# A long convolution with soft mixture-of-experts on one core: token sums in column quarters, combination in row quarters, experts with moving weights, spread weight loads

## The chip, the cores and the metric

The kernel runs on one NeuronCore of one Trainium2 chip, in f32 throughout. The metric is the device time of one execution in microseconds. Before the change it is 1391.36 us, the median of three runs (1389.31 to 1397.85).

## The reference

```python
def _attn_ref(x, h):                        # x (8, 5696, 128), h (5696, 128)
    Yf = np.fft.rfft(x, n=2 * S, axis=1) * np.fft.rfft(h, n=2 * S, axis=0)[None]
    return np.fft.irfft(Yf, n=2 * S, axis=1)[:, :S, :]

def _moe_ref(x, phi, w1, w2):               # x (45568, 128): 8 experts, 4 slots each, F = 1024
    logits = x @ phi                        # (45568, 32)
    d = softmax over the tokens (axis 0);  slot_input = d.T @ x
    slot_out[e] = relu(slot_input[e] @ w1[e]) @ w2[e]
    c = softmax over the slots (axis 1);   return c @ slot_out
```

(The two softmaxes are cut to a line each; both subtract the maximum and add 1e-9 to the sum.)

## The kernel before, in words

The convolution is a transform in two factors, 90 by 64, written as matmuls. The sequence is 89 rows of 64 columns (`R1 = 89`, `N2 = 64`), and a chunk is four columns from one end and the four mirrored ones from the other (`CH = 4`), so a batch has 8 chunks (`NJ`) and all of x has 64. The stages of the front are `stage_a` (matmul at L175, its result through DRAM as `f`), `stage_b1` (L205, the product with the transform of h on VectorE) and `stage_b2` (L241, its result through DRAM as `z`). `load_z` (L269) brings z back, `stage_c1` (L278) makes the convolved tokens y of a chunk, `stage_c2` transposes them (L295), `stage_c3` makes the logits (L303) and the token-wise softmax numerators, `stage_c4` transposes the combination weights and stores them to DRAM as `c_t` (L337, L342). Two chunks are a window: `window_max`, `window_top` (L358) and `window_row` (L376) keep a running maximum per slot over the tokens, and from it come the numerators d (L386, L389).

`dispatch` (from L394) sums d times y over the tokens of a chunk. Its weights are the 128 columns (4 token columns by 32 slots) of d, its moving operand the 512 columns (4 token columns by 128 channels) of y; only the four diagonal blocks of the 128 by 512 product are of use. A second matmul (L408) with the same weights and a column of ones gives the sums of d. At the end of a window five operations on VectorE (L418) merge the diagonal blocks and the sums into `acc`.

The order is written out by hand: the loop over `t` issues the pieces of several chunks in turn, with lags. The front runs in the steps t = 0 to 80, the token sums of chunk c in step t = c + 29, so that steps 29 to 80 hold both and steps 81 to 92 hold the token part alone. All loads and stores but four go through SyncE's queue (SP) in program order, eight of them in flight at most.

In step 81 (`t == last_front`) the front's memory is given back and all weights of the experts are loaded there, sixteen DMAs of 512 KB (L514, L515). After the loop the combination weights come back from DRAM (`cT`, L522, eight DMAs). The experts (L548, L556) take the weights `w1s` and `w2s` as stationary operand, 128 by 128 at a time, and 4 slots as moving operand. The result is spread into `sobd`, a block-diagonal operand of 128 by 512, and for each chunk two matmuls of 512 columns (L584) over 128 rows (4 token columns by 32 slots) give the output, which ScalarE and VectorE copy (L591, L589) and SP stores (L597).

Of the kernel before, what the change touches and what calls it, by code (L numbers as in the profile page):

```python
# [56 lines left out]
def kernel(  # L57
# [63 lines left out]
    aps = work.enter_context(tc.tile_pool(name="aps", bufs=1, space=PSUM))  # L121
# [131 lines left out]
    ybufs = [ypool.tile([P, 2 * CH, D], F32, name=f"y{i}") for i in range(NYB)]  # L253
# [19 lines left out]
    def stage_c1(c):  # L273
# [10 lines left out]
        nc.vector.tensor_tensor(out=y_[0:R1, 0:CH, :], in0=pv[0], in1=yo[:, :, :], op=AL.add)  # L284
        nc.vector.tensor_tensor(out=y_[0:R1, CH:2 * CH, :], in0=pv[0], in1=yo[:, :, :],
# [3 lines left out]
    def stage_c2(c):  # L289
        yt = cpool.tile([D, 2 * CH, R1], F32, name="yt", tag="yt")  # L290
        for f in range(2):
            p = bank()
            pv = p[:, 0:CH * R1].rearrange("p (n r) -> p n r", r=R1)
            for i in range(CH):
                nc.tensor.transpose(pv[:, i, :], ys[c][0:R1, f * CH + i, :], ident[0:R1, 0:R1])  # L295
            nc.scalar.activation(yt[:, f * CH:(f + 1) * CH, :], pv, AF.Copy)  # L296
        yts[c] = yt
# [96 lines left out]
    def dispatch(c):  # L394
        w, i = divmod(c, WC)
        if i == 0:
            accs[w] = (aps.tile([P, 512], F32, name="ap", tag="ap"),
                       aps.tile([P, 512], F32, name="sp", tag="sp"))
        ap_, sp_ = accs[w]
        d_ = ds.pop(c)  # L400
        y_ = ys.pop(c)
        for f in range(2):
            dv = d_[:, f * CH:(f + 1) * CH, :].rearrange("p n s -> p (n s)")
            first, last = i == 0 and f == 0, i == WC - 1 and f == 1
            nc.tensor.matmul(ap_[:, :], dv,  # L405
                             y_[:, f * CH:(f + 1) * CH, :].rearrange("p n d -> p (n d)"),
                             start=first, stop=last)
            nc.tensor.matmul(sp_[:, 0:1], dv, ones[:, 0:1], start=first, stop=last)  # L408
        if i < WC - 1:
            return  # L410
        parts = [(slice(q * NSL, (q + 1) * NSL), slice(0, D), ap_[q * NSL:(q + 1) * NSL,
                                                               q * D:(q + 1) * D])
                 for q in range(Q)] + [(slice(0, P), slice(D, D + 1), sp_[:, 0:1])]
        for r, cl, src in parts:
            if w == 0:
                nc.vector.tensor_copy(out=acc[r, cl], in_=src)
            else:
                nc.vector.scalar_tensor_tensor(out=acc[r, cl], in0=acc[r, cl],  # L418
                                               scalar=scales[w][r, 0:1], in1=src,
                                               op0=AL.mult, op1=AL.add)  # L420
# [27 lines left out]
    wait_b2 = []  # L448

    for t in range(steps):  # L450
# [57 lines left out]
        if t == last_front:  # L508
# [10 lines left out]
    tail = work.enter_context(tc.tile_pool(name="tail", bufs=1))  # L519
    cT = tail.tile([P, B * NJ, 2, R1], F32, name="cT")  # L520
    for b in range(B):
        nc.sync.dma_start(out=cT[:, b * NJ:(b + 1) * NJ, :, :].rearrange("p j f r -> p (j f r)"),  # L522
                          in_=cd[:, b * NJ:(b + 1) * NJ, :, :].rearrange("p j f r -> p (j f r)"))


    rep = wts.tile([P, NSL], F32, name="rep")
    for q in range(Q):
        r = slice(q * NSL, (q + 1) * NSL)
        nc.vector.tensor_copy(out=rep[r, :], in_=ident[r, r])
    p = bank()  # L530
    nc.tensor.matmul(p[0:NSL, 0:D + 1], rep[:, :], acc[:, :], start=True, stop=True)
# [9 lines left out]
    siT = wts.tile([P, NSL], F32, name="siT")  # L541
    nc.vector.tensor_copy(out=siT[:, :], in_=p[:, 0:NSL])
    hT = wts.tile([P, E, NFC, SPE], F32, name="hT")
    for e in range(E):
        hp = bank()
        hv = hp[:, 0:NFC * SPE].rearrange("p (t s) -> p t s", s=SPE)
        for k in range(NFC):
            nc.tensor.matmul(hv[:, k, :], w1s[:, e, k * P:(k + 1) * P],  # L548
                             siT[:, e * SPE:(e + 1) * SPE], start=True, stop=True)
        nc.scalar.activation(hT[:, e, :, :], hv, AF.Relu)  # L550
    soT = tail.tile([P, NSL], F32, name="soT")
    for e0 in range(0, E, 4):
        pp = [bank() for _ in range(4)]
# [4 lines left out]
        for e in range(e0, e0 + 4):  # L558
            nc.vector.tensor_copy(out=soT[:, e * SPE:(e + 1) * SPE], in_=pp[e - e0][:, 0:SPE])
    p = bank()  # L560
    nc.tensor.transpose(p[0:NSL, 0:D], soT[:, :], ident[:, :])
    so = tail.tile([NSL, D], F32, name="so")
    nc.vector.tensor_copy(out=so[:, :], in_=p[0:NSL, 0:D])
    rep2 = tail.tile([NSL, Q, NSL], F32, name="rep2")
    for q in range(Q):
        nc.vector.tensor_copy(out=rep2[:, q, :], in_=ident[0:NSL, 0:NSL])
    sobd = tail.tile([P, 2, Q, D], F32, name="sobd")
    nc.gpsimd.memset(sobd[:, :, :, :], 0.0)
    p = bank()
    nc.tensor.matmul(p[:, 0:D], rep2[:, :, :].rearrange("p q s -> p (q s)"), so[:, :],  # L570
                     start=True, stop=True)
    for q in range(Q):
        r = slice(q * NSL, (q + 1) * NSL)
        nc.vector.tensor_copy(out=sobd[r, 0, q, :], in_=p[r, 0:D])
        nc.scalar.activation(sobd[r, 1, Q - 1 - q, :], p[r, 0:D], AF.Copy)

    osp = work.enter_context(tc.tile_pool(name="osb", bufs=4))
    ov = out.rearrange("(b a n) d -> b a n d", b=B, n=N2)
    for c in range(B * NJ):
        b, j = divmod(c, NJ)  # L580
        o_ = osp.tile([R1, 2, CH, D], F32, name="o", tag="o")
        for f in range(2):
            p = bank()
            nc.tensor.matmul(p[0:R1, :], cT[:, c, f, :],  # L584
                             sobd[:, f, :, :].rearrange("p q d -> p (q d)"),
                             start=True, stop=True)
            pv = p[0:R1, :].rearrange("p (n d) -> p n d", d=D)
            if f:
                nc.vector.tensor_copy(out=o_[:, f, :, :], in_=pv)  # L589
            else:  # L590
                nc.scalar.activation(o_[:, f, :, :], pv, AF.Copy)  # L591
        gap = N2 - CH * (2 * j + 1)
        for r in (slice(0, SPLIT), slice(SPLIT, R1)):
# [33 lines left out]
```

## Time and profile before

| | us |
|---|---|
| median of 3 runs | 1391.36 |
| profiled execution | 1390.6 |
| its span | 1388.6 |
| PE busy | 1288.8 |
| VectorE busy | 732.7 |
| ScalarE busy | 501.1 |
| GpSimd busy | 306.2 |

PE is TensorE's matmuls, PEld its weight loads, which run beside matmuls. A group line gives line, engine, operation, result and operands, shapes (weights as rows*columns, then the moving operand), count, busy time, mean duration of one, and idle time before. Matmuls are pipelined: a duration includes the way through the array, so the spacing of matmuls is the busy time divided by the count. PEclk is the granted TensorE clock as a share of full speed, and the DMA share is the mean busy share of the 16 DMA engines.

### The profile page before, as it was taken

The numbers are of one execution on the slowest core, as the hardware profiler recorded it, in microseconds if no ns is written. First come the engines' busy times: TensorE is split into PE (matmuls) and PEld (weight loads), VectorE is DVE, ScalarE is ACT, GpSimd is POOL, SyncE is SP. The second block draws the span as 40 slices with busy tenths as digits, with TensorE's granted clock in tenths as the row PEclk, the third lists the DMA queues.
The fourth block names the chain that finished last, engine by engine and source line by source line (L and its number), as shares of the span: only waits on it lengthen the run. The fifth ranks groups of instructions, "written<-read, shape, count | busy, mean of one in ns | idle before, by whom it ended". The sixth has DMA issues, their size and how long they took to land.

```text
span 1388.6 us, 17824 instructions
## 1 busy us (share of the span) xinstructions
PE 1288.8 (93%) x5408; PEld 819.4 (59%) x5408; DVE 732.7 (53%) x1722; ACT 501.1 (36%) x1118; POOL 306.2 (22%) x346
## 2 busy tenths in 40 slices
PE   7588899999999999999999999999999659799998
PEld 2254565666666666666666666666676435496333
DVE  2045555665666666566666665666776424401443
ACT  3365343434343434433443334333333213101333
POOL 5233222222222322322232222221111101100000
PEclk9899999999999999999999999999999878756999
DMA  7799898877777677687767778766655753311776
GB/s 198 234 271 272 266 281 250 272 202 222 215 212 209 191 214 214 193 229 217 203 200 213 215 200 218 219 200 175 178 159 158 210 156 80 120 60 43 216 213 203
DMA packets 197532, 277.73 MB, mean 200 GB/s; under 512 B 18072, under 2 KB 134040, under 8 KB 197439
## 3 DMA queue, kind: packets, MB, share of 16 engines
q1 hardware_dynamic: 196863, 276.14, 68.2%
q8 instruction: 45, 0.74, 0.2%
q10 hardware_dynamic: 576, 0.46, 0.1%
q14 instruction: 48, 0.39, 0.1%
HBM read 147.09 MB, written 129.43 MB: 199 GB/s over the span
## 4 chain that ended last, share of the span: by engine, by line
PE 82%; DMA 8%; DVE 4%; SPq 2%; ACT 1%; issue 1%; POOL 1%; POOLq 0%; ACTq 0%; DVEq 0%
PE bank L278 17%; PE bank L175 15%; PE bank L205 11%; PE bank L241 10%; PE bank L584 8%; PE ap L405 7%; PE bank L303 5%; PE bank L295 3%; DMA gt<-f 3%; DMA f<-fst 2%; PE bank L556 2%; PE bank L548 2%; DMA zc<-z 1%; SPq L514 1%; PE sp L408 1%
## 5 line engine op out<-in xcount | busy, mean ns | idle before, releaser
L175 PE MATMUL bank<-x,s 128*128 128x512 f32 x576 | 283.5, 618 | 12.2 <-POOL x L164 6.9
L278 PE MATMUL bank<-zc,i 128*128 128x512 f32 x512 | 238.8, 610 | 23.1 <-DMA zc<-z 23.1
L205 PE MATMUL bank<-gt,wt 128*128 128x256 f32 x810 | 216.0, 390 | 27.5 <-DMA gt<-f 26.8
L164 POOL TENSOR_TENSOR x<-xc 89x512 f32<-89x512 f32 x144 | 182.4, 1267 | 219.4 <-PE bank L175 168.7
L177 ACT ACTIVATE fst<-bank 90x512 f32<-90x512 f32 x288 | 160.1, 587 | 173.5 <-PE bank L175 61.9
L205 PEld LDWEIGHTS bank<-gt,wt 128*128 128x128 f32 x810 | 152.2, 193 | 116.6 <-issue 82.2
L223 DVE TENSOR_TENSOR pr<-bank,Hr 128x512 f32<-128x512 f32 (+1 forms) x184 | 124.1, 674 | 170.8 <-PE bank L205 170.8
L241 PE MATMUL bank<-yf,vt 128*128 128x256 f32 x720 | 187.0, 381 | 5.9 <-DVE yf L229 4.3
L244 ACT ACTIVATE zst<-bank 128x512 f32<-128x512 f32 (+1 forms) x184 | 107.3, 583 | 227.9 <-PE bank L241 175.9
L278 PEld LDWEIGHTS bank<-zc,i 128*128 128x128 f32 x512 | 94.1, 194 | 121.9 <-issue 89.2
L175 PEld LDWEIGHTS bank<-x,s 128*128 128x128 f32 x576 | 103.8, 195 | 99.4 <-issue 78.6
L284 DVE TENSOR_TENSOR y<-bank,yo 89x512 f32<-89x512 f32 x64 | 44.0, 687 | 213.1 <-PE bank L278 198.9
L317 POOL TENSOR_TENSOR ct<-L,rm 89x256 f32<-89x256 f32 x64 | 39.2, 612 | 530.0 <-DVE rm L315 391.8
L241 PEld LDWEIGHTS bank<-yf,vt 128*128 128x128 f32 x720 | 136.6, 191 | 29.6 <-issue 6.1
L405 PE MATMUL ap<-y,d 128*128 128x512 f32 x256 | 144.0, 651 | 2.5 <-ACT d L389 2.5
L223 DVE TENSOR_TENSOR pi<-bank,Hi 128x512 f32<-128x512 f32 (+1 forms) x184 | 122.9, 668 | 0.0
L584 PE MATMUL bank<-sobd,cT 128*89 128x512 f32 x256 | 111.5, 598 | 2.4 <-issue 2.4
L303 PEld LDWEIGHTS bank<-phi,yt 128*89 128x89 f32 x1024 | 91.0, 159 | 9.6 <-issue 3.8
L408 PEld LDWEIGHTS sp<-ones,d 128*128 128x128 f32 x256 | 51.1, 200 | 65.6 <-issue 65.6
L303 PE MATMUL bank<-phi,yt 128*89 128x32 f32 x1024 | 88.4, 240 | 0.3 <-ACT yt L296 0.3
L227 DVE TENSOR_TENSOR yf<-pr,pi 128x256 f32<-128x256 f32 (+1 forms) x184 | 82.1, 446 | 6.4
L584 PEld LDWEIGHTS bank<-sobd,cT 128*89 128x89 f32 x256 | 40.8, 160 | 72.5 <-issue 72.2
(77 smaller groups left out, 1133.3 us busy)
## 6 DMA issues: line engine op xcount, KB each, us to landing
f<-fst SPq DMA_DIRECT2D x144, 360.0 KB
gt<-f SPq DMA_DIRECT2D x396, 128.0 KB
zc<-z SPq DMA_DIRECT2D x64, 720.0 KB
z<-zst SPq DMA_DIRECT2D x176, 256.0 KB
xc<-in_x_dram SPq DMA_DIRECT2D x64, 320.0 KB
out_dram<-o SPq DMA_DIRECT2D x64, 320.0 KB
c_t<-cst SPq DMA_DIRECT2D x64, 89.0 KB
cT<-c_t SPq DMA_DIRECT2D x8, 712.0 KB
```

What stands on the lines that cost most here:

```text
L164: nc.gpsimd.tensor_tensor(out=y_[0:R1, :, :], in0=t_[:, 0, :, :], in1=t_[:, 1, ::-1, :], op=AL.subtract if comp else AL.add)
L175: nc.tensor.matmul(p[:, :], s1[:, tab[G], :], src[:, :, :].rearrange("p n d -> p (n d)"), start=True, stop=True)
L177: nc.scalar.activation(st[:, :, G, :], p[0:N1, :].rearrange("p (n d) -> p n d", d=D), AF.Copy)
L205: nc.tensor.matmul(p[:, q * 256:(q + 1) * 256], wt[:, 2 * i + q, :], t_[:, q, :, :].rearrange("p c d -> p (c d)"), start=True, stop=True)
L223: nc.vector.tensor_tensor(out=t[:, 0:n, :, :], in0=pv[:, 0:n, :, :], in1=H[:, 2 * i:2 * i + n, :].unsqueeze(2).broadcast_to([P, n, 2, D]), ...
L227: nc.vector.tensor_tensor(out=y_[:, 0:n, 0, :], in0=pr[:, 0:n, 0, :], in1=pi[:, 0:n, 1, :], op=AL.subtract)
L241: nc.tensor.matmul(p[:, q * 256:(q + 1) * 256], vt[:, 2 * i + q, :], y_[:, q, :, :].rearrange("p c d -> p (c d)"), start=True, stop=True)
L244: nc.scalar.activation(st[:, 0:n, :], p[:, 0:n * 256].rearrange("p (q c) -> p q c", q=n), AF.Copy)
L278: nc.tensor.matmul(p[:, :], i1[:, tabs[q], :], t_[:, o, :, q, :], start=(q == 0), stop=(q == 1))
L303: nc.tensor.matmul(p[0:R1, i * NSL:(i + 1) * NSL], yt[:, i, :], phi[:, :], start=True, stop=True)
L405: nc.tensor.matmul(ap_[:, :], dv, y_[:, f * CH:(f + 1) * CH, :].rearrange("p n d -> p (n d)"), start=first, stop=last)
L584: nc.tensor.matmul(p[0:R1, :], cT[:, c, f, :], sobd[:, f, :, :].rearrange("p q d -> p (q d)"), start=True, stop=True)
```

## The change

**Token sums in column quarters.** The rows of y get one more column, set to 1 once (`D + 1` = 129 wide). Each of the four token columns becomes a matmul of its own with 32 columns of d as weights, whose result goes to its own 32 partitions of one bank: column quarters of the array. The diagonal blocks alone are computed, the ones column gives the sums, and one operation merges a window. The bank is now double.

**Weight loads spread.** w1 and w2 of one expert are loaded at the end of each of the steps 81 to 88, with the combination weights of one batch in each of the steps 81 to 87; the last batch follows after the loop.

**Experts with moving weights.** The slot inputs are laid out with zeros (`siz`), 32 columns per expert in which only the expert's own 4 are filled, and are the stationary operand, with w1 moving, 512 columns at a time; four experts go to four column quarters. The hidden layer is transposed on PE, and its 32-column pieces are the weights against which w2 moves, 128 columns at a time.

**Combination in row quarters.** The slot outputs stand four times, once per 32 partitions (`so4`). For each token column a matmul over 32 rows, with 89 columns of `cT` as weights and 128 moving columns, writes to one of four banks: row quarters of the array. Two chunks go together, with one copy per bank.

```diff
-    aps = work.enter_context(tc.tile_pool(name="aps", bufs=1, space=PSUM))
+    aps = work.enter_context(tc.tile_pool(name="aps", bufs=2, space=PSUM))
...
-    ybufs = [ypool.tile([P, 2 * CH, D], F32, name=f"y{i}") for i in range(NYB)]
+    ybufs = [ypool.tile([P, 2 * CH, D + 1], F32, name=f"y{i}") for i in range(NYB)]
...
+    for t_ in ybufs:
+        nc.vector.memset(t_[0:R1, :, D:D + 1], 1.0)
...
         for f in range(2):
-            dv = d_[:, f * CH:(f + 1) * CH, :].rearrange("p n s -> p (n s)")
-            first, last = i == 0 and f == 0, i == WC - 1 and f == 1
-            nc.tensor.matmul(ap_[:, :], dv,
-                             y_[:, f * CH:(f + 1) * CH, :].rearrange("p n d -> p (n d)"),
-                             start=first, stop=last)
-            nc.tensor.matmul(sp_[:, 0:1], dv, ones[:, 0:1], start=first, stop=last)
+            for q in range(Q):
+                nc.tensor.matmul(ap_[q * NSL:(q + 1) * NSL, 0:D + 1], d_[:, f * CH + q, :],
+                                 y_[:, f * CH + q, :], start=(i == 0 and f == 0),
+                                 stop=(i == WC - 1 and f == 1))
...
+            nc.vector.scalar_tensor_tensor(out=acc[:, :], in0=acc[:, :],
+                                           scalar=scales.pop(w)[:, 0:1], in1=ap_[:, 0:D + 1],
+                                           op0=AL.mult, op1=AL.add)
...
-            for e in range(E):
-                nc.sync.dma_start(out=w1s[:, e, :], in_=moe_w1[e])
-                nc.sync.dma_start(out=w2s[:, e, :, :],
-                                  in_=moe_w2[e].rearrange("(c p) d -> p c d", p=P))
+        e = t - last_front
+        if 0 <= e < E:
+            nc.sync.dma_start(out=w1s[:, e, :], in_=moe_w1[e])
+            nc.sync.dma_start(out=w2s[:, e, :, :],
+                              in_=moe_w2[e].rearrange("(c p) d -> p c d", p=P))
+            if e < B - 1:
+                load_c(e)
...
-        for k in range(NFC):
-            nc.tensor.matmul(hv[:, k, :], w1s[:, e, k * P:(k + 1) * P],
-                             siT[:, e * SPE:(e + 1) * SPE], start=True, stop=True)
...
+            for q in range(Q):
+                nc.tensor.matmul(p[q * NSL:(q + 1) * NSL, :], siz[:, g * Q + q, :],
+                                 w1s[:, g * Q + q, f0:f0 + FH], start=True, stop=True)
...
+                nc.tensor.transpose(p[:, k * P:(k + 1) * P],
+                                    hid[:, g, (k0 + k) * P:(k0 + k + 1) * P], ident[:, :])
...
         for k in range(NFC):
-            for e in range(e0, e0 + 4):
-                nc.tensor.matmul(pp[e - e0][:, 0:SPE], w2s[:, e, k, :], hT[:, e, k, :],
-                                 start=(k == 0), stop=(k == NFC - 1))
+            for q in range(Q):
+                nc.tensor.matmul(sop[q * NSL:(q + 1) * NSL, 0:D],
+                                 hidT[:, g, k, q * NSL:(q + 1) * NSL], w2s[:, g * Q + q, k, :],
+                                 start=(g == 0 and k == 0), stop=(g == EG - 1 and k == NFC - 1))
...
-        for f in range(2):
-            p = bank()
-            nc.tensor.matmul(p[0:R1, :], cT[:, c, f, :],
-                             sobd[:, f, :, :].rearrange("p q d -> p (q d)"),
-                             start=True, stop=True)
+        pq = [bank() for _ in range(Q)]
+        for i in range(PC):
+            for f in range(2):
+                k = (i * 2 + f) * D
+                for q in range(Q):
+                    r = slice(q * NSL, (q + 1) * NSL)
+                    nc.tensor.matmul(pq[q][0:R1, k:k + D], cT[r, c0 + i, f, :], so4[r, :],
+                                     start=True, stop=True)
```

The order of the program shows at three places what moves. First TensorE in a combined step, around one dispatch (`ap` is the bank of the token sums, `sp` that of the sums of d, `y` and `d` a chunk's tokens and numerators; the shape is that of the result). Before:

```order
L303 MATMUL bank<-phi,yt 89x32 x8
L175 MATMUL bank<-x_99,s_92 128x512 x2
L205 MATMUL bank<-gt,wt 128x256 x2
L241 MATMUL bank<-yf,vt 128x256 x2
L337 MATMUL bank<-ident,ct 128x89 x2
L405 MATMUL ap<-y_104,d_110 128x512
L408 MATMUL sp<-ones,d_110 128x1
L405 MATMUL ap<-y_104,d_110 128x512
L408 MATMUL sp<-ones,d_110 128x1
L175 MATMUL bank<-x_98,s_92 128x512 x2
L205 MATMUL bank<-gt,wt 128x256 x2
```

And with the change:

```order
L305 MATMUL bank<-phi,yt 89x32 x8
L175 MATMUL bank<-x_99,s_92 128x512 x2
L205 MATMUL bank<-gt,wt 128x256 x2
L241 MATMUL bank<-yf,vt 128x256 x2
L339 MATMUL bank<-ident,ct 128x89 x2
L405 MATMUL ap<-y_104,d_110 32x129 x8
L175 MATMUL bank<-x_98,s_92 128x512 x2
L205 MATMUL bank<-gt,wt 128x256 x2
```

Four matmuls of a dispatch have become eight smaller ones; everything around them stands as it did (line numbers move by two).

Second, SyncE's queue from step 81 on (`zc` is z coming back, `c_t` the store of combination weights, `w1s` and `w2s` the experts' weights). Before, from the middle of the sixteen weight loads:

```order
L514 DMA w1s<-in_moe_w_dram 128x1024
L515 DMA w2s<-in_moe_w_dram 128x8x128
L514 DMA w1s<-in_moe_w_dram 128x1024
L515 DMA w2s<-in_moe_w_dram 128x8x128
L514 DMA w1s<-in_moe_w_dram 128x1024
L515 DMA w2s<-in_moe_w_dram 128x8x128
L269 DMA zc_107<-z 90x2x1024
L342 DMA c_t<-cst 128x178
L269 DMA zc_106<-z 90x2x1024
L342 DMA c_t<-cst 128x178
```

And with the change, from the first of them:

```order
L344 DMA c_t<-cst 128x178
L518 DMA w1s<-in_moe_w_dram 128x1024
L519 DMA w2s<-in_moe_w_dram 128x8x128
L447 DMA cT<-c_t 128x1424
L271 DMA zc_107<-z 90x2x1024
L344 DMA c_t<-cst 128x178
L518 DMA w1s<-in_moe_w_dram 128x1024
L519 DMA w2s<-in_moe_w_dram 128x8x128
L447 DMA cT<-c_t 128x1424
L271 DMA zc_106<-z 90x2x1024
```

Each z load now has three loads ahead of it in its step, where one had sixteen and the others none; the reads of `cT` have moved from behind the loop into the steps.

Third, TensorE from the last dispatch to the end. Before:

```order
L408 MATMUL sp<-ones,d_108 128x1
L531 MATMUL bank<-acc,rep 32x129
L540 MATMUL bank<-ident,si 128x32
L548 MATMUL bank<-siT,w1s 128x4 x64
L556 MATMUL bank<-hT,w2s 128x4 x64
L561 MATMUL bank<-ident,soT 32x128
L570 MATMUL bank<-so,rep_10157 128x128
L584 MATMUL bank<-sobd,cT 89x512 x128
```

And with the change:

```order
L405 MATMUL ap<-y_105,d_108 32x129 x8
L534 MATMUL bank<-acc,rep_10075 32x129
L543 MATMUL bank<-ident,si 128x32
L559 MATMUL bank<-w1s,siz 32x512 x16
L570 MATMUL bank<-ident,hid 128x128 x16
L578 MATMUL ap<-w2s,hidT 32x128 x64
L584 MATMUL bank<-so,rep_10075 128x128
L600 MATMUL bank<-so_10214,cT 89x128 x512
```

64 matmuls of 4 columns against w1 have become 16 of 512 and 16 transposes, the 64 against w2 are now 128 columns wide, and the combination has 512 matmuls of 128 columns in place of 128 of 512.

More of the change, by code (lines that the diff above doesn't have):

```diff
@@ L396, in dispatch @@
         if i == 0:
[L397 to L399 removed]
+            accs[w] = aps.tile([P, 512], F32, name="ap", tag="ap")
+        ap_ = accs[w]
         d_ = ds.pop(c)
@@ L561 @@
[L561 to L568, printed above, removed]
-    p = bank()
-    nc.tensor.matmul(p[:, 0:D], rep2[:, :, :].rearrange("p q s -> p (q s)"), so[:, :],
-                     start=True, stop=True)
```

118 lines of the change are left out of this document (66 added, 52 removed).

## The prediction

> **What bounds the kernel now.** I read the page first, then busy time by stretches, then groups by shape, then the chain of waits and the timelines. The profiled execution took 1390.6 us (span 1388.6 us and 2.0 us around it); the median of the three runs shown is 1391.36 us, so the sum below starts from 1390.6. About 1% (14 us) is what a measurement of this kernel can tell from no change.
>
> The page: busy time, then in 40 slices the TensorE clock that was granted and the DMA share.
>
> ```profile
> span 1388.6 us, 17824 instructions
> PE 1288.8 (93%) x5408; PEld 819.4 (59%) x5408; DVE 732.7 (53%) x1722; ACT 501.1 (36%) x1118; POOL 306.2 (22%) x346
> ...
> PEclk9899999999999999999999999999999878756999
> DMA  7799898877777677687767778766655753311776
> ```
>
> PE is the bound on average, but the clock sags between slices 31 and 36, so the end of the program must be read apart from its middle. Busy time by stretches does that:
>
> ```profile
> core 0: us, PE busy (x) PEld busy (x) DVE busy (x) ACT busy (x) POOL busy (x), PEclk, DMA share, GB/s
> 1091.11:1123.75 32.64, 9.91 (x48) 5.67 (x45) 6.62 (x21) 4.11 (x12) 3.23 (x5) 0.65 1.04 302
> 1123.75:1183.90 60.15, 55.01 (x261) 33.51 (x262) 26.65 (x74) 15.42 (x41) 10.15 (x16) 0.87 0.28 74
> 1183.90:1209.30 25.40, 21.33 (x91) 12.34 (x89) 7.93 (x26) 6.13 (x17) 6.14 (x9) 0.82 0.19 66
> 1213.35:1240.47 27.12, 27.12 (x129) 27.12 (x129) 0.00 (x0) 1.38 (x7) 0.00 (x0) 0.51 0.25 103
> 1240.47:1267.80 27.33, 27.31 (x128) 27.22 (x128) 1.13 (x7) 0.20 (x1) 0.00 (x0) 0.50 0.00 1
> 1272.29:1383.90 111.61, 111.51 (x256) 40.77 (x256) 43.28 (x63) 38.13 (x65) 0.00 (x0) 0.99 0.69 203
> 230.00:1071.00 841.00, 833.40 (x3854) 554.73 (x3853) 537.12 (x1265) 326.05 (x727) 210.94 (x246) 1.00 0.72 206
> ```
>
> Four stages, four limits. In 230 to 1071 (the 52 steps, t = 29 to 80, in which the front and the token sums run together) PE works 833 of 841 us at full clock: PE time taken away there comes off the end. In 1091 to 1124 the DMA engines are full (1.04, 302 GB/s) and PE works 9.9 of 32.6 us. In 1213 to 1268 (experts) PE is busy throughout, at half clock, with nothing moving. In the combination from 1272 PE is busy throughout and the DMA engines at 0.69.
>
> **The prices.** Groups by shape; count, then busy us and mean ns of one:
>
> ```profile
> L405 PE MATMUL ap<-y,d 128*128 128x512 f32 x256 | 144.0, 651 | 2.5 <-ACT d L389 2.5
> L584 PE MATMUL bank<-sobd,cT 128*89 128x512 f32 x256 | 111.5, 598 | 2.4 <-issue 2.4
> L303 PE MATMUL bank<-phi,yt 128*89 128x32 f32 x1024 | 88.4, 240 | 0.3 <-ACT yt L296 0.3
> ...
> L548 PE MATMUL bank<-siT,w1s 128*128 128x4 f32 x128 | 27.1, 351 | 0.3 <-DVE siT L542 0.3
> ```
>
> The code issues 128 matmuls on L584 and the trace has 256: each f32 matmul is two passes, each with its own weight load. A pass of 512 columns costs 111.5/256 = 0.436 us, 0.85 ns a column: 0.110 us for 129 columns, 0.109 for 128. L548 is bound by its weight loads: 27.1/128 = 0.212 us for 128 columns at clock 0.51, so 0.83 ns a column at full clock, 0.027 us for 32. L303 gives at most 88.4/1024 = 0.086 us for a load of 89 columns and L548's rate 0.074: I take 0.08.
>
> What no row shows is two passes at once on different quarters of the array. The ends are: none at all, and four at a time. Between them I take this mechanism: the two passes of one matmul use the same quarter and follow each other, while the second pass of one runs beside the first of the next matmul, which sits on another quarter, once that one's weights are in. A matmul then costs one pass and one weight load instead of two passes. I choose it because in all these rows PE takes instructions in program order, and that order puts both passes of a quarter together.
>
> **Token sums.** One dispatch now, in the chain of waits:
>
> ```profile
> 1131.16 0.89 PE ap L405 x2
> 1132.06 0.12 PE sp L408 x2
> 1132.17 0.97 PE ap L405 x2
> 1133.14 0.12 PE sp L408 x2
> ```
>
> That is 2.10 us. After, 8 matmuls of 129 columns on 32-column weights: 8 x (0.110 + 0.027) = 1.10 us; no overlap gives 16 x 0.110 = 1.76, or 2.19 if the small weight loads stop being hidden too; four at a time gives a quarter of 1.76 and some 0.1 to start, 0.55. I take 1.10: 1.00 us off each of 52 PE-bound steps, **52 us** (ends -5 and 81). The single merge in place of five on DVE and the 129-wide rows of y lie on an engine that works 537 of 841 us: nothing, covered by PE; without that cover the wider rows still move the same 512 elements.
>
> A rule speaks against this part. The row first: an L405 pass occupies 0.56 us of PE (144.0/256) but is recorded as 651 ns, and L584's 0.436 as 598, so up to 0.16 us of a pass drains beside its successor. The Trainium skill, TensorEngine Tiling (Array Packing), Key Properties, states that changing the tiling mode drains TensorE; no run here shows it yet. By that rule each of the two switches of a dispatch would expose this drain; without it the sum stays as it is.
>
> **Last steps.** PE's timeline at the first and last combined step, and SP's issue of the z load between:
>
> ```profile
> 1091.11 3.63 PE L278 MATMUL bank<-zc,i 128*128 128x512 f32 x8
> ...
> 1123.75 6.01 PE L278 MATMUL bank<-zc,i 128*128 128x512 f32 x8 [21.43 <-DMA zc<-z]
> ...
> 1183.91 4.90 PE L278 MATMUL bank<-zc,i 128*128 128x512 f32 x8
> ```
>
> ```profile
> 1112.58 2.49 SPq L269 DMA_DIRECT2D zc<-z  x1
> ```
>
> The z load stands behind the sixteen weight loads on SP, issues at 1112.6, 21 us after the first step began, and PE idles 21.4 us for it. These seven steps take 92.8 us. Sizes:
>
> ```profile
> zc<-z SPq DMA_DIRECT2D x64, 720.0 KB
> ...
> out_dram<-o SPq DMA_DIRECT2D x64, 320.0 KB
> c_t<-cst SPq DMA_DIRECT2D x64, 89.0 KB
> cT<-c_t SPq DMA_DIRECT2D x8, 712.0 KB
> w1s<-in_moe_w_dram SPq DMA_DIRECT2D x8, 512.0 KB
> w2s<-in_moe_w_dram SPq DMA_DIRECT2D x8, 512.0 KB
> ...
> out_dram<-o SPq DMA_DIRECT2D x64, 36.0 KB
> ```
>
> After, each step moves 512 + 512 + 712 + 720 + 89 KB = 2.6 MB, at 302 GB/s 8.6 us. The z load now waits on SP behind one w1, one w2 and one cT load, and behind it stand the c_t store and the next step's loads; PE waits for z. I allow 1 us for it to land: 9.6 us a step, against PE's own 10.0 (60.15/6, at clock 0.87) less the dispatch's 1.0. So DMA sets it: 7 x 9.6 = 67 us, **25 us** saved (ends: 9, if load and clock dips add up to 12 us a step; 30, if PE's 9.0 holds). The four dispatches after 1183.9 give 1 us each, **4 us**. The cT loads moved forward were hidden behind the experts and save nothing by themselves: their 5.8 MB take 19 us at 302 GB/s, and 31 us of experts would still cover that.
>
> **Experts.** From the last dispatch (1209.3) to the first combination matmul (1272.3) it is 63 us. After: the same 4 us to the slot inputs; 16 matmuls of 512 columns, 16 x (0.436 + 0.027) = 7.4; an eviction 0.9; 16 transposes x 0.109 = 1.7; an eviction 0.9; 64 x (0.109 + 0.027) = 8.7; copies and the replication 1.6: 25 us at full clock. The clock was 0.82 before this stage and 0.50 in it, so I add 6 us for a slow first third: 31, **32 us** saved. Without overlap PE takes 14 + 14 and the stage 43; with full overlap 21.
>
> **Combination.** From 1272.3 to the end is 116.3 us, 4.8 of it outside PE's 111.5. After, 512 matmuls of 128 columns on 89-column weights: 512 x (0.109 + 0.08) = 97, with 4.8 it is 101.6: **15 us** saved. No overlap: 1024 x 0.109 = 111.6, nothing. Full overlap: 1024 weight loads x 0.08 = 82, 30 us. Two other floors lie below: 64 x 356 KB = 23.3 MB at 302 GB/s is 77 us, and evictions and issues:
>
> ```profile
> L597 SPq DMA_DIRECT2D out_dram<-o x128: 317/340/436, 1276.4 to 1385.0; - x128
> L591 ACT ACTIVATE o<-bank x64: 592/593/593, 1274.3 to 1383.0; 89x512 f32<-89x512 f32 x64
> L589 DVE COPY o<-bank x64: 686/687/690, 1275.7 to 1383.9; 89x512 f32<-89x512 f32 x64
> ```
>
> 64 x 0.687 = 44 us on DVE, 128 x 0.34 = 44 us on SP. A new wait: each pair of chunks takes four of six banks, so the next pair's third matmul waits for the first eviction. A pair's PE time (3.0 us) covers the two evictions of each engine (1.4 us); at four at a time it would not, and about 0.7 us per pair shows, still under the weight loads.
>
> **The sum.** 52 + 25 + 4 + 32 + 15 = 128 us: 1390.6 - 128 = **1263 us**.
>
> **Rivals.**
> 1. Four quarters at a time: 81 + 31 + 42 + 30 = 184, **1207 us**. For it: a weight load already runs inside another pass (the L584 loads are 40.8 us within 111.5). Against: both passes of a quarter stand together in program order. The Trainium skill, TensorE: Matmul & The Clock Gate, Measured speedup vs the span model, gives 2.38 for three column tiles and 3.07 for four row tiles, without saying that this holds for two-pass f32; no row here shows it. Chance 0.20.
> 2. Quarters do not overlap: 18 (0.34 x 52) + 26 + 20 + 0 = 64, **1327 us**. For it: every row now is one pass behind the other. Chance 0.22.
> 3. Overlap as forecast, but each switch of shape drains the array: 64 dispatches x 2 x 0.16 = 21 us, **1284 us**. Chance 0.12.
> 4. Slower: the combination runs at half clock. In the expert windows PE is busy throughout and still granted 0.50, so being busy does not earn the full clock. If quarter-array passes neither overlap nor keep the clock, the combination takes 223 us in place of 112, and 1327 + 112 = **1439 us**. It decides from clock 0.63 down (112/0.63 = 176, the 64 us given back). Against: L584's passes stream back to back at 0.99, and the row-quarter passes stream as densely, unlike L548's four columns. Chance 0.05; with the clock near the break-even, no change, 0.03.
>
> The forecast keeps 0.38. **Range** 1205 to 1330: it reaches down to rival 1 and up to rival 2, since both are ends of the one unknown price; the forecast's own range is 1240 to 1290. Faster by over 1%: 0.38 + 0.20 + 0.22 + 0.12 = 0.92; within 1%: 0.03; slower: 0.05.
>
> **What would show it.** Right: L405 at about 1.1 us per dispatch and steps near 15.2 us in the middle; L280's wait for zc down from 21 us to a few; experts near 31 us; the combination near 102 us with the DMA share near 0.8. Wrong: a dispatch at 1.8 us or more and a combination of 112 us (no overlap); 0.55 and 85 (full overlap); granted clock near 0.5 in the last 100 us; or z waits of several us in each of the last steps, which would mean that spreading only divided the stall.

## The result, and the profile after

The changed kernel takes 1271.6 us (median of four runs, 1269.29 to 1272.35), the kernel before 1391.39 us on the same chip (four runs, 1389.31 to 1397.85). The ratio is 0.9129, with an interval of 0.9097 to 0.9161: faster, and 9 us above the predicted 1263. The profiled execution took 1269.29 us (span 1267.5), so its 121.3 us less than the one before (1390.6) are what has to be found again in the stages. The page after:

```profile
span 1267.5 us, 19943 instructions
PE 1118.3 (88%) x6607; PEld 737.5 (58%) x6607; DVE 700.6 (55%) x1588; ACT 498.3 (39%) x1110; POOL 305.7 (24%) x345
...
PEclk9899999999999999999999999999999898876755
DMA  7889998977777787777777877787666546771788
```

The clock still sags at the end, and now stays low to the last slice, where the DMA engines have become busy. Busy time by the five stretches that answer to those of before (combined steps, the seven last steps, the last dispatches, experts, combination):

```profile
core 0: us, PE busy (x) PEld busy (x) DVE busy (x) ACT busy (x) POOL busy (x), PEclk, DMA share, GB/s
230.00:1040.00 810.00, 774.81 (x4266) 519.19 (x4265) 515.72 (x1165) 328.49 (x730) 209.97 (x245) 0.99 0.75 213
1057.00:1134.90 77.90, 55.95 (x365) 34.28 (x363) 28.77 (x80) 20.37 (x56) 15.40 (x24) 0.80 0.82 241
1134.90:1155.94 21.04, 14.91 (x121) 9.83 (x121) 6.47 (x19) 5.48 (x16) 3.85 (x6) 0.66 0.15 45
1155.94:1172.86 16.92, 13.37 (x182) 7.21 (x182) 5.67 (x16) 2.37 (x4) 0.00 (x0) 0.72 0.14 45
1172.86:1267.50 94.64, 61.76 (x1024) 51.55 (x1024) 41.11 (x64) 34.48 (x64) 0.00 (x0) 0.59 0.81 248
```

PE was busy for 833 of 841 us in the combined steps; now it idles there for 35 of 810. In the combination it was busy throughout; now it works 62 of 95 us. Two stages have lost PE as their bound. Against the forecast's terms, where a stage's saving is taken from the starts of the first matmul of each step (L278 before, L280 after) in the two traces:

| stage | forecast, us saved | measured |
|---|---|---|
| steps before the token sums (t < 29) | 0 | 2 |
| combined steps | 52 | 32 |
| seven last steps | 25 | 15 |
| last dispatches | 4 | 4 |
| experts | 32 | 46 |
| combination | 15 | 22 |
| sum | 128 | 121 |

The total came out because the errors had both signs: 30 us too much in the first two large terms, 21 too little in the last two. That they nearly cancel is luck; only the term of the last dispatches came out by itself, and that not for the reason given (below).

**A dispatch.** The chain of waits gives the new price (start, us, what), with the stage A that follows; below it stands the group of all dispatch passes:

```profile
611.75 0.58 PE ap L405 x16
612.33 1.91 PE bank L175 x4
```

```profile
L405 PE MATMUL ap<-y,d 128*32 128x129 f32 x1024 | 42.5, 286 | 1.2 <-ACT d L391 1.2
```

0.58 us for 16 passes, where the forecast had 1.10 and four at a time 0.55. In the trace's single records the passes start in fours, 7 ns apart (611.678, 611.685, 611.691, 611.698), and the next four 0.11 to 0.13 us later, the time of one pass of 129 columns. All four quarters run at once. By the difference from 2.10 us that should have given 1.52 us in each of 52 steps, 79 us.

**The new wait.** 47 of them are not there. TensorE's waits (engine, line and releaser: us in total, times, longest), before and after:

```profile
PE bank L278 <- DMA zc<-z: 23.1, 2, 21.4
...
PE bank L376 <- ACT dn L382: 7.1, 5, 1.6
...
PE bank L376 <- DVE dg L369: 2.2, 2, 1.2
```

```profile
PE bank L378 <- DVE dg L371: 35.7, 26, 2.7
...
PE bank L600 <- ACT o L608: 21.6, 31, 1.8
PE bank L378 <- ACT dn L384: 14.4, 5, 3.1
PE bank L280 <- DMA zc<-z: 8.7, 6, 3.0
```

The matmul of `window_row` (L376, now L378) waited 9.3 us in all and waits 50.1 now. The timeline of one window shows how. Before:

```profile
552.18 0.20 DVE L360 TENSOR_REDUCE top<-bank 128x1 f32<-128x89 f32 x1
...
552.41 0.62 DVE L362 TENSOR_TENSOR top<-top 128x1 f32<-128x1 f32 x1
552.42 1.96 PE L175 MATMUL bank<-x,s 128*128 128x512 f32 x4
...
553.14 0.23 DVE L369 TENSOR_SCALAR dg<-ident,top 128x32 f32<-128x32 f32 x1
...
554.22 0.27 PE L376 MATMUL bank<-dg,ones 128*89 128x32 f32 x2
...
554.52 1.26 POOL L164 TENSOR_TENSOR x<-xc 89x512 f32<-89x512 f32 x1 [1.51 <-PE bank L376]
```

After:

```profile
535.38 0.65 PE L405 MATMUL ap<-y,d 128*32 128x129 f32 x16
...
535.96 1.98 PE L175 MATMUL bank<-x,s 128*128 128x512 f32 x4
...
537.16 0.20 DVE L362 TENSOR_REDUCE top<-bank 128x1 f32<-128x89 f32 x1
...
537.39 0.62 DVE L364 TENSOR_TENSOR top<-top 128x1 f32<-128x1 f32 x1
...
538.08 1.26 POOL L164 TENSOR_TENSOR x<-xc 89x512 f32<-89x512 f32 x1
538.12 1.25 DVE L371 TENSOR_SCALAR dg<-ident,top 128x32 f32<-128x32 f32 x1
...
539.52 0.31 PE L378 MATMUL bank<-dg,ones 128*89 128x32 f32 x2 [1.58 <-DVE dg L371]
```

Between the matmul that hands the window's maxima to VectorE (L358, now L360) and the one that needs `dg` back, TensorE's program holds a dispatch and a stage A. When the dispatch took 2.10 us, VectorE's chain (maximum, running maximum, difference, `dg`) was done within them. Now the cover is 1.5 us shorter and the chain ends last. It also grew: before, GpSimd's fold (L164) waited 1.51 us for TensorE and started after `dg`; now stage A is over earlier, the fold starts 0.04 us ahead of `dg`, and `dg` takes 1.25 us in place of 0.23 (in 12 of the 32 windows). From t = 72 on, when there is no stage A left between the two, the wait is about 3 us, and the matmuls behind it run at about half speed (the granted clock is 0.50 from 963.9 to 967.3 us):

```profile
963.53 0.31 PE L378 MATMUL bank<-dg,ones 128*89 128x32 f32 x2 [2.94 <-ACT dn L384]
963.68 1.82 PE L205 MATMUL bank<-gt,wt 128*128 128x256 f32 x4
...
965.30 1.91 PE L241 MATMUL bank<-yf,vt 128*128 128x256 f32 x4
```

L205 and L241 take 1.11 and 1.03 us for four passes elsewhere. Up to t = 81 the waits on L378 sum to 37.0 us against 8.1 before, and five such slow stretches cost some 1.7 us each (an estimate: 3.4 us at half clock): 29 + 8 = 37 of the 47.

**Experts and combination.** The chain of waits from the last slot inputs to the first combination matmuls:

```profile
1159.58 6.46 PE bank L559 x32
1166.04 1.90 PE bank L570 x16
1167.94 3.67 PE ap L578 x128
```

The combination's groups (after the second bar: idle time of the engine before them, and what ended it):

```profile
L600 PE MATMUL bank<-so,cT 32*89 32x128 f32 x1024 | 61.8, 387 | 22.0 <-ACT o L608 21.6 <-DVE so L587 0.4
...
L606 DVE COPY o<-bank 89x512 f32<-89x512 f32 x64 | 41.1, 682 | 43.8 <-PE bank L600 27.5 <-DMA out_dram<-o 15.4 <-issue 1.0
L608 ACT ACTIVATE o<-bank 89x512 f32<-89x512 f32 x64 | 34.5, 588 | 54.9 <-PE bank L600 36.6 <-DMA out_dram<-o 16.9 <-ACT o L608 1.4
```

The copies wait 32 us for stores to give their buffers back, which they did not do before. TensorE waits for the copies, and the DMA engines stand at 0.81.

### The profile page after: what moved, and what is told of

It is laid out like the page before. It is cut to its first block, busy times and chain, and to the rows that moved or that the text cites. A ratio compares the mean times of both kernels' runs of the same rounds, so it can differ in the third digit from the quotient of the medians.

```text
span 1267.5 us, 19943 instructions
## 1 busy us (share of the span) xinstructions
PE 1118.3 (88%) x6607; PEld 737.5 (58%) x6607; DVE 700.6 (55%) x1588; ACT 498.3 (39%) x1110; POOL 305.7 (24%) x345
## 4 chain that ended last, share of the span: by engine, by line
PE 67%; DMA 12%; DVE 11%; ACT 3%; SPq 2%; issue 2%; POOL 1%; POOLq 0%; ACTq 0%; DVEq 0%
PE bank L280 18%; PE bank L205 13%; PE bank L175 12%; PE bank L241 10%; PE bank L305 6%; DMA zc<-z 4%; DMA gt<-f 4%; PE bank L297 3%; DMA f<-fst 3%; PE bank L600 2%; DMA out_dram<-o 2%; DVE pr L223 1%; SPq L616 1%; PE ap L405 1%; DVE pi L223 1%
## 5 line engine op out<-in xcount | busy, mean ns | idle before, releaser
L280 PE MATMUL bank<-zc,i 128*128 128x512 f32 x512 | 246.6, 626 | 8.9 <-DMA zc<-z 8.7
L205 PE MATMUL bank<-gt,wt 128*128 128x256 f32 x810 | 218.8, 394 | 27.6 <-DMA gt<-f 27.6
L205 PEld LDWEIGHTS bank<-gt,wt 128*128 128x128 f32 x810 | 153.4, 195 | 118.0 <-issue 86.7
L164 POOL TENSOR_TENSOR x<-xc 89x512 f32<-89x512 f32 x144 | 182.3, 1266 | 158.6 <-PE bank L175 142.2
L241 PE MATMUL bank<-yf,vt 128*128 128x256 f32 x720 | 189.0, 384 | 4.8 <-DVE yf L229 3.4
L280 PEld LDWEIGHTS bank<-zc,i 128*128 128x128 f32 x512 | 96.9, 200 | 113.3 <-issue 99.7
L241 PEld LDWEIGHTS bank<-yf,vt 128*128 128x128 f32 x720 | 137.6, 192 | 29.6 <-issue 5.4
L600 PE MATMUL bank<-so,cT 32*89 32x128 f32 x1024 | 61.8, 387 | 22.0 <-ACT o L608 21.6
L227 DVE TENSOR_TENSOR yf<-pr,pi 128x256 f32<-128x256 f32 (+1 forms) x184 | 77.2, 419 | 6.4
L229 DVE TENSOR_TENSOR yf<-pr,pi 128x256 f32<-128x256 f32 (+1 forms) x184 | 75.9, 413 | 0.0
L322 ACT ACTIVATE ct<-ct 89x256 f32<-89x256 f32 x64 | 26.7, 417 | 122.4 <-POOL ct L319 122.4
L600 PEld LDWEIGHTS bank<-so,cT 32*89 32x89 f32 x1024 | 51.5, 233 | 32.1 <-ACT o L608 31.5
```

Source lines behind the costliest of these rows:

```text
L164: nc.gpsimd.tensor_tensor(out=y_[0:R1, :, :], in0=t_[:, 0, :, :], in1=t_[:, 1, ::-1, :], op=AL.subtract if comp else AL.add)
L205: nc.tensor.matmul(p[:, q * 256:(q + 1) * 256], wt[:, 2 * i + q, :], t_[:, q, :, :].rearrange("p c d -> p (c d)"), start=True, stop=True)
L227: nc.vector.tensor_tensor(out=y_[:, 0:n, 0, :], in0=pr[:, 0:n, 0, :], in1=pi[:, 0:n, 1, :], op=AL.subtract)
L229: nc.vector.tensor_tensor(out=y_[:, 0:n, 1, :], in0=pr[:, 0:n, 1, :], in1=pi[:, 0:n, 0, :], op=AL.add)
L241: nc.tensor.matmul(p[:, q * 256:(q + 1) * 256], vt[:, 2 * i + q, :], y_[:, q, :, :].rearrange("p c d -> p (c d)"), start=True, stop=True)
L280: nc.tensor.matmul(p[:, :], i1[:, tabs[q], :], t_[:, o, :, q, :], start=(q == 0), stop=(q == 1))
```

## The experiments

The first theory (**A**): every quarter works by itself, a dispatch costs 0.58 us, and what is missing in the front is the uncovered VectorE chain in `window_row`. Its rivals stand with each run. Each ratio is to the kernel before, on the same chip. Edits are to the changed kernel unless said.

### e1_row_late: window_row two places later

```diff
         r = chunk(3)
-        if r is not None and r % WC == 0:
-            window_row(r // WC)
         slot_b()
         c1 = chunk(1)
         if c1 is not None:
             stage_c2(c1)
         if c is not None:
             stage_c1(c)
+        if r is not None and r % WC == 0:
+            window_row(r // WC)
         slot_b()
```

> The changed kernel with window_row moved behind stage_c1 in its step. Theory A (the matmul of window_row, L378, waits 50.1 us in total for the maximum's chain on VectorE, because the dispatch that stood ahead of it has shrunk from 2.1 to 0.6 us): the wait is covered by some 6 us of matmuls, combined pairs of steps go from 32.2 to about 30.3 us, and the time falls by 45 to 65 us, to about 1215. Rival B (the front lost its gain to the clock or to DMA latency, not to this wait): the wait goes away but comes back elsewhere, 1255 to 1275. Rival C (the later d keeps dispatch waiting for ScalarE): L405 waits more than 20 us in total.

1237.2 us (1235.0 to 1240.63), ratio 0.8901 (0.888 to 0.8922). The wait on L378 went from 50.1 to 2.2 us, and the lead over the kernel before at t = 82 (how much sooner the step begins) from 34 to 75 us: of the 79, 70 have now come in the combined steps. Rival B falls, and so does C (L405 waits 7.3 us for ScalarE). But of the 40 us gained there only 31 reached the end of the profiled execution (34 by the medians), and the expected 1215 was missed. TensorE's waits, and the seven last steps:

```profile
PE bank L280 <- DMA zc<-z: 27.8, 6, 6.7
...
PE bank L378 <- DVE dg L371: 2.2, 1, 2.2
```

```profile
1016.50:1102.70 86.20, 52.76 (x361) 31.61 (x361) 28.01 (x80) 19.44 (x55) 14.06 (x22) 0.79 0.76 220
```

The waits for z rose from 8.7 to 27.8 us, while the DMA engines were at 0.76: they were not full, z was late in the queue. SP's timeline shows the order. Two steps stand close together, each with w1, w2 and cT ahead of z, and then nothing is issued for 15 us:

```profile
1018.42 0.36 SPq L518 DMA_DIRECT2D w1s<-in_moe_w_dram  x1
...
1024.92 0.42 SPq L518 DMA_DIRECT2D w1s<-in_moe_w_dram  x1
...
1026.59 0.85 SPq L271 DMA_DIRECT2D zc<-z  x1
1042.17 0.34 SPq L344 DMA_DIRECT2D c_t<-cst  x1
```

So A holds for the front, and it had not named the price in the tail.

### e2_dg_scalar: dg made by ScalarE

```diff
-        nc.vector.tensor_scalar(out=dg[:, :], in0=ident[:, 0:NSL], scalar1=top[:, w:w + 1],
-                                scalar2=None, op0=AL.mult)
+        nc.scalar.activation(dg[:, :], ident[:, 0:NSL], AF.Copy, scale=top[:, w:w + 1])
```

> The changed kernel with the small product dg (128x32) done on ScalarE instead of VectorE, order otherwise as it is. Theory A1 (in 13 windows VectorE's dg takes 1.25 us in place of 0.23 because GpSimd's 1.26 us fold runs at the same time, and L378 waits 1.6 us there in place of 0.4): those waits shrink to about 0.4, the time falls by 10 to 20 us to about 1255, the waits of 2.7 us in the last steps stay. Rival (the 1.25 us only follows the wait, or the queue's order makes it): no change, 1266 to 1275.

1254.16 us (1253.29 to 1260.16), ratio 0.9036 (0.9009 to 0.9062). The wait fell to 29.3 us, the lead at t = 82 rose from 34 to 53 us:

```profile
L377 PE MATMUL bank<-dg,ones 128*89 128x32 f32 x64 | 11.9, 270 | 29.3 <-ACT dg L371 29.3
```

So the long `dg` was a part of the new wait, and the rest of VectorE's chain the other. ScalarE's `dg` takes 0.32 us in all 32 windows. How often `dg` is long differs between the runs, even where the combined steps are the same program, and the gain goes with it: with 12 long ones (changed kernel), 12 (e3_quarter_major), 8 (e4_sums_only), 6 (e8_wide_stores), 4 (e7_few_stores) and none (this run), the combined steps take 32, 31, 35, 39, 42 and 49 us less than before, about 1.4 us for each.

### e3_quarter_major: both matmuls of a quarter together

```diff
-        for f in range(2):
-            for q in range(Q):
+        for q in range(Q):
+            for f in range(2):
```

> The changed kernel with the two halves of a chunk as the inner loop of a dispatch, so that two matmuls on the same quarter stand next to each other. Theory D (passes overlap only with neighbours on other quarters in program order): a dispatch goes from 0.58 to about 1 us, L405's busy time from 42.5 to about 60 to 70 us; the time changes by less than 10 us, since L378 waits for VectorE anyway. Rival E (the chip regroups passes over a long window): a dispatch stays near 0.58 us and L405 at 42 to 45 us.

1271.97 us (1263.7 to 1275.53), ratio 0.9141 (0.9104 to 0.9178): no change, and the busy time of L405 is in the range of rival E.

```profile
L405 PE MATMUL ap<-y,d 128*32 128x129 f32 x1024 | 44.2, 288 | 1.2 <-ACT d L391 1.2
```

With four passes of one quarter in a row in the program, the passes still start in fours (611.531, 611.544, 611.557, 611.571, then 611.665), now 13 ns apart. The records don't name the quarter, but four passes of 129 columns that start within 0.04 us, when one alone takes 0.11, can't be on one. In the changed kernel two passes of the program lie between the first passes of neighbouring quarters and the starts are 7 ns apart; here it is four, and 13 ns. That fits a list that is read in order at some 3.3 ns a pass while each quarter works off its own passes, but no run shows that mechanism by itself. The theory that neighbours in the program must sit on different quarters (60 to 70 us) falls. The Trainium skill, TensorE: Matmul & The Clock Gate, in Part 3 under The mechanism, states of matmuls on different tiles that they start and end strictly in program order; by that rule the second to fourth of these starts would belong to the first quarter, and this run speaks against it for such a list.

### e4_sums_only: the token sums alone, in the kernel before

The edit takes the hunks on `aps`, on the width of y and in `dispatch` from the change, and nothing else:

```diff
         for f in range(2):
...
+            for q in range(Q):
+                nc.tensor.matmul(ap_[q * NSL:(q + 1) * NSL, 0:D + 1], d_[:, f * CH + q, :],
+                                 y_[:, f * CH + q, :], start=(i == 0 and f == 0),
+                                 stop=(i == WC - 1 and f == 1))
```

> The kernel before with the token sums in column quarters alone. Theory A: the front gains 32 us as in the changed kernel and the end 4 to 5 us, the stall of 21 us, the experts and the combination stay: 1391 - 36 = about 1355, L376 waiting about 50 us. The forecast's own term was 56 us: 1335. Full overlap without any new wait would give 1305.

1349.15 us (1344.5 to 1350.7), ratio 0.9699 (0.9677 to 0.9721), 6 below the 1355 of A and far from 1305, full overlap without a new wait. The wait comes with the token sums and with nothing else of the change:

```profile
PE bank L378 <- DVE dg L371: 29.1, 24, 2.7
...
PE bank L378 <- ACT dn L384: 14.4, 5, 3.1
```

### e5_spread_only: the spread loads alone, in the kernel before

```diff
-            for e in range(E):
-                nc.sync.dma_start(out=w1s[:, e, :], in_=moe_w1[e])
...
+        e = t - last_front
+        if 0 <= e < E:
+            nc.sync.dma_start(out=w1s[:, e, :], in_=moe_w1[e])
...
+            if e < B - 1:
+                load_c(e)
```

> The kernel before with the weight loads and the cT loads spread over the last steps, nothing else. Theory A: as in the changed kernel the stall of 21 us goes and some waits for z of 1 to 3 us come instead, so the seven steps take about 76 to 78 us in place of 92.8: 1391 - 16 = 1375. The forecast's term of 25 us would give 1366; if spreading only divides the stall, 1385 to 1391.

1375.45 us (1372.13 to 1377.76), ratio 0.9871 (0.9829 to 0.9912): 17 us less by the medians, as A expected, and 15 in the seven steps themselves, where the forecast had 25. The stall of 21.4 us is gone, and then the steps with loads give 5 us back (the lead falls from 21.3 to 16.3 us by t = 89), with waits for z in five of them (7.4 us).

### e6_z_first: z ahead of the weights, and window_row late

On top of e1_row_late, from step 81 on z is loaded as soon as stage C1 has freed its buffer, which puts it on SP ahead of that step's weights:

```diff
-        if chunk(-1) is not None:
+        if chunk(-1) is not None and t <= last_front:
             load_z(chunk(-1))
...
             stage_c1(c)
+        if t >= last_front:
+            load_z(t - LAG_C + 2)
```

> The first experiment (window_row late, 1237 us) and, from step 81 on, each z load issued right after stage_c1, so ahead of the step's weight loads on SyncE's queue. Theory F (the waits for z, 27.8 us there, come from the order of the queue: w1, w2 and cT of one step stand ahead of z and take 6 us, while the DMA engines are idle between the bursts): the waits fall under 5 us, the clock dips after them go, and the time falls by 25 to 35 us to about 1207. Rival G (bandwidth: each step's 2.6 MB have to pass anyway): the waits stay above 20 us or turn up at w1s, 1230 to 1240.

1211.4 us (1208.72 to 1213.59), ratio 0.8699 (0.8668 to 0.873), 60 us below the changed kernel. The waits for z fell from 27.8 to 2.6 us, and the seven last steps from 86.2 to 59.4 us. The program moves the same bytes as before; 16.9 MB of them now pass within these steps, where it was 19.0 (GB/s times time):

```profile
1015.70:1075.10 59.40, 50.47 (x360) 30.58 (x360) 26.16 (x72) 18.71 (x54) 13.42 (x21) 0.91 1.00 284
```

8.5 us a step at a DMA share of 1.00. The order in the queue, and not the bytes, had held these steps: the 2.1 MB that now pass elsewhere are worth 7 of the 27 us at 284 GB/s.

### e7_few_stores: one pair in eight stored

Seven eighths of the output are not written.

```diff
-        for i in range(PC):
+        for i in range(PC if c0 % 16 == 0 else 0):
```

> The changed kernel with the output of one pair of chunks in eight stored, so that seven eighths of the output are not written. If the stores bound the combination (94.6 us for 23.3 MB), the pairs go back to the 1.78 us of the first ones and the combination takes about 60 us, 1235 in all. If PE at half clock (2.17 us a pair) and the turnover of six banks (0.5 us) bound it, it stays at 2.7 us a pair, 86 us, and 1260.

One execution, 1222.71 us, 49 less than the changed kernel. It reached the combination 11 us sooner, in steps that the edit does not touch, with a long `dg` in 4 windows in place of 12; the rest is the combination itself. That stage, from its first matmul to the end:

```profile
1162.00:1220.20 58.20, 40.38 (x1024) 33.32 (x1024) 41.10 (x64) 34.48 (x64) 0.00 (x0) 1.00 0.18 53
```

58.2 in place of 94.6 us, at clock 1.00 in place of 0.59, with the same matmuls and copies. Both the time and the low clock of this stage come with the stores. Banks and copies alone allow 1.8 us a pair.

### e8_wide_stores: longer rows, fewer DMAs

The two chunks of a pair are laid side by side, and a pair is stored with two DMAs whose rows are 4 KB, in place of four with 2 KB:

```diff
-        for i in range(PC):
-            b, j = divmod(c0 + i, NJ)
-            gap = N2 - CH * (2 * j + 1)
+        b, j = divmod(c0, NJ)
+        gap = N2 - CH * (2 * j + PC)
...
+            v = bass.AP(tensor=v.tensor, offset=v.offset,
+                        ap=[v.ap[0], [gap * D, 2], [1, PC * CH * D]])
```

> The changed kernel with the two chunks of a pair laid out side by side, so that a pair is stored by two DMAs with rows of 4 KB instead of four with rows of 2 KB; same bytes. If the number of DMAs or of rows holds the stores at 262 GB/s and 0.86 share, the combination falls from 94.6 us to 80 to 87, the time by 8 to 14 us to about 1260. If bytes alone count, or PE's clock, it stays within 4 us of 1271.

1259.35 us (1250.99 to 1266.9), ratio 0.9043 (0.8988 to 0.9098). The combination itself took 93.1 us:

```profile
1168.10:1261.20 93.10, 56.20 (x1024) 46.95 (x1024) 41.10 (x64) 34.48 (x64) 0.00 (x0) 0.67 0.84 252
```

1.5 us less than the changed kernel's, though there are half as many DMAs with rows twice as long: neither number is what holds the stage, and the 80 to 87 us did not come. The profiled execution is 6 us shorter than that of the changed kernel, and the other 5 us arose ahead of the combination (it began at 1168.1 in place of 1172.9 us), in steps that the edit does not touch. There `dg` was long in 6 windows and not in 12, and L378 waited 41.2 us and not 50.1. That the wide spread of the four runs has the same reason is likely but not shown.

### e9_z_first_wide: e6 and e8 together

> The version of e6_z_first (running maximum's row later, z ahead of the weights) with the stores of e8_wide_stores (a pair of chunks laid side by side, two DMAs of 4 KB rows). If the bytes of the stores bound the combination, it keeps its 93 us (e8: 93.07, e6: 94.4) and the time is that of e6_z_first less 1 to 2 us: 1209 to 1211 us. If the larger part of the 12 us by which e8_wide_stores stood under the changed kernel came from the stores, the time is about 1199 us.

1211.19 us (1207.71 to 1215.9), ratio 0.8704 (0.8676 to 0.8732): the same as e6_z_first. The combination took 89.8 us against its 94.4, but began 2.7 us later. So longer rows are worth 1.5 us in one pair of runs and 4.6 in the other, and the 12 us that e8_wide_stores seemed to bring were not a property of the stores.

## Why the prediction held, and where its steps failed

**The price of a quarter (failed).** The step that failed is "PE takes instructions in program order, and that order puts both passes of a quarter together", from which overlap of two followed. The quarters run four at a time, as rival 1 had it: 0.58 us a dispatch (forecast 1.10), 3.7 us for the passes against w2 (forecast 8.7), and 6.5 us for the 32 against w1 (forecast 7.4) although the granted clock was 0.56 there. e3_quarter_major shows that the order within a dispatch does not matter: program order was no reason for the price. The rows of before could not show this; the mistake was to put 0.38 on a mechanism that only the program's order spoke for.

**Token sums (52 forecast, 32 measured).** With the right price the term would have been 79; 47 were lost. The step that failed is "nothing, covered by PE": it looked on VectorE for the merge and the wider rows only, and did not ask what VectorE does for `window_row` in the time that a dispatch had covered. e1_row_late gave back 38 of the 47 in these steps, e4_sums_only shows that the loss belongs to this part of the change alone, and e2_dg_scalar that about 17 of it come from `dg` and the engine that makes it. 5 more are the switch into quarters ahead of each dispatch (below), which the 0.58 us does not hold; some 4 stay open.

**Last steps (25 forecast, 15 measured; the mechanism held, the size was off).** 77.9 us where 67 were forecast. The order in SP's queue was named, with 1 us for z to land behind its three loads. In these steps the changed kernel waits 5.7 us for z (five times), about what was allowed, and 10.9 us for `dg`, which was not; with 5.2 us for `c`, as before, and 56.0 of work that is the stage. e6_z_first reaches 59.4 us with the DMA engines full, so the forecast's 8.6 us a step was close to the floor of the transfers, and the 18 us between the two were the order in the queue and the new wait, but for the bytes that moved out of these steps.

**Last dispatches (4, and 4).** As forecast, but by luck: TensorE works 6.4 us less (four dispatches at 1.5, not 1.0) and idles 2.1 us more. It is 21.0 us where 21.4 were expected, at clock 0.66.

**Experts (32 forecast, 46 measured).** 16.9 us. The way to the slot inputs (3.6 us), the transposes (1.9) and the copies behind (1.3) cost about what was said (4, 1.7 and 1.6); the passes on quarters cost less, and the two evictions do not show in the chain. Of the 6 us for a slow first third about 3 are there: the passes against w1 take 6.5 us, where 8 times 0.436 is 3.5.

**Combination (15 forecast, 22 measured).** 94.6 us where 101.6 were forecast and 86 with full overlap. Both priced TensorE, which does not bound the stage: its work is 62 us, and the stores, named as a floor of 77 us, hold it at 248 GB/s. e7_few_stores shows it: without most of them it takes 58 us. So the 102 us forecast was near for a reason that does not hold. What in the stores sets 248 GB/s is open: the DMA engines are at 0.81, and no run shows whether more than four output buffers would fill them. The new wait for banks that was put at 0.7 us a pair is 0.46 to 0.52 in the first pairs.

**The rivals.** Of rival 1 the mechanism was right and the sum (1207) wrong, because it had counted no new waits; e6_z_first, which removes two of them, ends 4 us above it, though not by the same terms (33 us in the last seven steps, 22 in the combination where the rival had 30). Rivals 2 and 3 fall: there is overlap, and a switch costs about 0.09 us. From the last transpose (L339) to the first pass it is 0.17 us from start to start, where it was 0.08 in the kernel before, and from the last pass to the next matmul 0.20, where it was 0.11. The Trainium skill, TensorEngine Tiling (Array Packing), Key Properties, states that a change of tiling mode drains TensorE; the trace agrees, at about 0.18 us for both switches of a dispatch, 12 us in 64 of them, where rival 3 had 21; the overlap more than pays for them. Rival 4 was half right: the clock in the combination did fall to 0.59, with the waits for stores and not for want of overlap, and PE had time to spare. (Two figures of the prediction are slightly off, and change nothing: L548's loads take 0.84 ns a column, not 0.83, and 112/0.63 is 178, not 176.)

## What to carry over

When work that is taken off the bounding engine stood between a hand-over to another engine and the use of its answer, write down that other engine's chain and what now covers it; here half of the gain went back into one wait, and moving one call a few places later returned it. A load that the next step needs belongs ahead of bulk loads in the same queue, even where the bytes fit. And price every stage by its next bound as well: once matmuls cost a quarter, the stores were the stage.

## What the hardware showed that was not expected

- **A VectorE operation held by GpSimd's.** `dg` (128 by 32) takes 0.23 us, but 1.25 us in the 12 of 32 windows in which the fold of GpSimd (1.26 us) started 0.04 us before it; it then ends 0.04 us after the fold. In three windows in which the fold started 0.11 us after `dg`, `dg` kept its 0.23. The running maximum (128 by 1) stands beside a GpSimd product that starts 2 to 8 ns ahead of it: in most windows it takes 0.62 us and the product 0.61, in the others 0.16 and the product 0.65, in the kernel before too. So either of the two can be the one that is held. The Trainium skill, SBUF — State Buffer, SBUF: two separate sides, states that VectorE, in its two-port modes and in operations with two inputs in SBUF, shares a pair of ports with GpSimd under an exclusive lock, which the first takes for its whole instruction; the 1.25 us agree; for the maximum the recorded starts, a few ns apart, do not tell which was first. ScalarE's `dg` (0.32 us) in e2_dg_scalar was not held.
- **Half clock after short waits.** A wait of 2.9 us was followed by 3.4 us at a granted clock of 0.50, and by four passes in 1.82 us in place of 1.11. In the combination the longest wait is 1.8 us (31 in all, 21.6 us), and the granted clock is 0.59; in e7_few_stores, with the longest at 0.5 us (31, 15.7 us), it is 1.00:

```profile
PE bank L600 <- ACT o L608: 15.7, 31, 0.5
```

The waits take about the same share of the stage in both (23 and 27%), so it is not their sum; that it is their length is not shown.

- **A quarter costs nothing beyond its share.** In e7_few_stores 1024 passes of 128 columns with weight loads of 89 columns take 40.4 us, 0.039 us each with the ends of each pair, where 0.08 was taken for a weight load alone. Within the first pair the fours start 0.109 us apart, the price of one pass of 128 columns: the loads of the quarters run side by side as well, and don't show.
